# Loads, scale steps, filler products and the written-out order at the start of a fused attention and MLP kernel

## The chip, the core and the metric

The kernel runs on one core of a Trainium2 chip. The metric is the device time in microseconds of one execution. The notes use the profile's short names: PE is the matrix engine, DVE the vector engine, ACT the scalar engine, POOL the general-purpose engine, SP the queue that issues most DMAs.

## The reference

One input `x` (2048 tokens of 512 numbers) goes through a layer norm and then through two branches whose results are added to `x`. Branch A is attention with 32 heads of 16, in 4 segments of 512 tokens, with a memory carried from segment to segment. Branch B is a second layer norm and an MLP with 1792 hidden numbers.

```python
for s in range(N):
    qs, ks, vs = q[:, :, s], k[:, :, s], v[:, :, s]
    p = _softmax(qs @ ks^T * scale + mask)           # causal, inside the segment
    a_dot = p @ vs
    num, den = phi(qs) @ M, phi(qs) @ z + 1e-6       # memory of the segments before
    outs.append(g * num / den + (1.0 - g) * a_dot)
    M, z = M + phi(ks)^T @ vs, z + sum(phi(ks))
A = concat(outs) @ wo
B = gelu(layernorm(xn) @ w1 + b1) @ w2 + b2          # 512 -> 1792 -> 512
return x + A + B
```

## The kernel before, in words

Matrix work is done in pairs of 16-bit numbers: a value is split in a high and a low part, and a product is three matmuls (high by high, high by low, low by high; `split3`, L583). Before a weight can be split it is scaled by a power of two that follows from its sum of squares. The sum comes from ACT squares (`w_square`, L351) or from the trace of a product on PE (`w_trace`, L380 on PE, L382 on DVE); `qk_scale` and `w_scale` add it up over the partitions with a product by ones (L394, L412), take the exponent bits on DVE (`exponents`, L386) and form the factors from them (`power`, L390); `w_split` makes the high part on ACT (L445) and the low part on DVE (L446), or spreads the piece over POOL, ACT and POOL (L448, L450, L452). Raw weights lie in the same buffer as the split ones, two pieces further on.

The work is cut in steps with short names, and a step's instructions are issued when its key comes up. The tokens are handled in halves of 256 rows, `X` (load, statistics, root on POOL, normalization; L472, L483, L532, L534) and `Xt` (transposition, L561 on PE, L564 on ACT, L565 on DVE). A unit `i` is one segment and one group of 8 heads, 16 units in all. `Tp` is the product of q or k of unit 0 with the first 256 rows, `T` the product with the rest or with all 512; `V` is the product for v of 128 rows (12 matmuls of 512 columns). `M` (L741 on PE, L748 on DVE) finds the row maxima of unit `i`'s logits in 10 jobs, `R` turns them (L754 on PE), and they go through DRAM into the operand of `S` (L783, exponentials on ACT, L790). `pv` (L817) multiplies by v, `D` and `e` (L583 with w1, and L926) are the MLP's two layers, `out` (L944, added on DVE in L947) the last product, and `st` the store. `W` are products of the identity with itself that nobody reads (L501). `C` and `Cb` form the rows that undo the first layer norm's scale (L510, L524, L525).

The order is written out by hand in the string ORDER: each character names a stream of steps, and the next step of that stream is issued. So every engine runs its instructions in the order in which the string names their steps, and every DMA of SP likewise. The string BANKS gives each product its PSUM bank.

Of the kernel before, what the change touches and what calls it, by code (L numbers as in the profile page):

```python
# [19 lines left out]
P = 128  # L20
D = 512
# [11 lines left out]
NW = 8  # L33
# [25 lines left out]
def streams():  # L59
# [15 lines left out]
    for m in PARTS:  # L75
        put("loads", *[("wl", m, k) for k in range(LOADS[m])])
        if m == "qk":
            put("loads", ("hold",))
        if m == "v":
            put("loads", ("par",))  # L80
# [57 lines left out]
    "oamakrkkhbckkkk0h0bihehceddhff220ff22qhjkk2n1h1662gkkrp6237s7lg3k783w8th88999!x9u#k!w7#9$4$vRRv9R$9!3#R!#%k4J5"  # L138
    "WxkR%&RRzzz%(S%%Lz&WTzXU%Vst)L(uzz3%Tk)U&LvVYY(zTvU)z)VTz&L)Y(UYi3-YzVY*YYYk*K+-,X4zzyz**J5Y+YYYz-,6AAY-*5RAAA"
    "aBRB-RzzCBC.K.+C*C/,*A.+kAzRRR,zAA:WkRzAWz/.sRt.uzSy:TjRBwUBxBR.C.CCVCvDAbATEBFGAURwAvVARBRHxJYz/zCBCCTUICKzXA"  # L140
    "zYYzA:/VcYTURAzzsXBAz:VtiAYBvBSYYRzTzCCUuCCdDYvYz;YeEYVJT;FUVRfyRYfRY;;aATAzYbRUAzGAVYTBRcYAHzzdUBVBYeIYRSzz<z"
    "YYCCCKCz=AzYYYff>TUYYYAaAzjBsAAVtz<bYROBR<wTuyCNBCxCCA=AvDUY>RBREJPsVTYYFUGVTAuAvAHYtiwYzBzCxCBCICAzYNYRUAzAVB"
    "RYAzAvRzzzcvBCOSCBTUCCzzRYYLRDVYYEzFYzz<GzyYLYLHezATUIAMZAAAVQLBzBBWzCTCXKCCUzVAzdMJAzzsAAAMRBzMByBtCCuTCKCADA"
    "EPOwBFxAAvAvRNYZfYZfYBGUQRJBRYWCiVHKCICCzAYYzAAYBRAAzBSOYPXYYBzzzTsYzUztCuCaCCzzVYTwjxRUVTDRYYvbRzERUvVJFTURcY"
    "yWdYORYRYYSYNzeAAVYRiYTYBXYAzzYYRZUYAzAGYVRBTzzCKHBCIUCCAABVTzRWRAAXzRAUzzffRYBjVYYYTSzUQYysPBaVCCCtCADAEYBYwu"
    "AFTAGAYYxNYYBYBYQYCHCvObCICAAARvPJURABzBABszzzCCtCCLVuLTzcUVDvzzwxETdLeFzzzLGfRYYzfRHNUyVRTUVYRAAAYBRvYAAzIYMY"
    "ZBzzCBCCSKiCRAWzzaMYTYUAVzARJYbzcABABMQBYzzTUzZCCVCCTUKXsuMzYJRtDRPEyWwFxYAAAYYVGHTRQYUAABOvNIVYBRPBCCKXvCCAZA"
    "zYBYYzAAYBRAzzSjBesTzzzCCtduCUVCTDYURYYREwYzzvzxVYRTFGYJYUVYfYzRNZTyUVYYvRHRYYAAABYRYOfzAWzYSYYTYRUzAzBYYRQzzC"
    "IBCCCVzzAszAtTzURRYVAATAROWPvBUzRwRNBYyVYSXROBYCCTUXCVxCDTjAAYYYEYAFAABYGRYRYBRBHKvCIUCCCAzVATYzYYizzAsBzUzAVR"
    "QzARRTzBzBzCtCSCCPUDwLYExFYVvzGLyTYLNvLHIAAAMYzUAVzTYUYMzBzAYVMZQzZzzBCTCUOBCCAAstzzzYYYPwBWYzYAAABYVxYZNyvYBM"  # L150
    "CTCUCCvAABAYRRRDAEAzVBRFBGHRRQPWRCTCCICAjzAYUYsztAAWYXYVYzzAwvxzzBSzBXCBCTCUCDYVYTUYVYTvURYEzzVRTRYYNRRZzRRYYS"
    "FOYzUVzyATYYRUzAAGBVYYYYTHABXAzRBYUzzCCIVCCzzTAYRYUWVzAARYAzTARYBUVzBRRCSCBTUCCQDEXyVYYAAYTYFYGABPYABAYYBYHYCC"
    "UICCYAVAABYATYYBYAQUYYBCVCTUCCDEVYFYYGHYYIYYYYYYMMMZMZZZ"
# [4 lines left out]
    "01234567012345614526371052671034261705342617035426107356420735264071526540715402675430125673012657320614527036"  # L158
    "41752036475126347512034715623471625437164325741362534612054612704631720476231547361204367120436712430624751062"
    "41705241705617205436172436017236017620347620341576203145762031457632145176320475163204751632407513624057136240"  # L160
    "57162401572431507243107624531762541736257431602576403157640315640371564072561473265104765104736510427651024702"
    "63517305264137052641702614702351470623154706234710536427153642751036427513642735167340516735401564730215643725"
    "61437516437054317605431760543761054361205437205413725024513740256137425061742506314506310473152047361052170365"
    "27052431670524315627053614270361423761024671025671032567120536127410253645130243510624351067243167524316754236"
    "17542356417023564127035641270356120356142705164270514521670421657210465201476537206143720614206173540267302547"
    "03251403142650314261540356410235641027536142753641275036127503461250"
# [17 lines left out]
def infini_mixer_kernel(ctx: ExitStack, tc: tile.TileContext, x, wq, wk, wv, wo, beta, w1, b1, w2, b2, out):  # L184
# [71 lines left out]
    def col(j):  # L256
        return sc[:, j:j + 1]
# [25 lines left out]
    def w_load(m, k):  # L283
# [27 lines left out]
        elif m[0] == "1":  # L311
            f0, n = (0, FH) if m == "1a" else (FH, FH - 2)
            d = flat("1")[:, 1024 + 512 * f0:1024 + 512 * (f0 + n)].rearrange("p (f k c) -> p f k c", f=n, k=KT)
            for r in (2 * k, 2 * k + 1):
                Q.dma_start(d[:, :, r, :], w[P * r:P * r + P, P * f0:P * (f0 + n)].rearrange("p (f c) -> p f c", f=n))
        else:
            f0, n = {"v": (0, 2), "o": (0, 2), "2a": ((0, 4), (4, 3))[k % 2], "2b": (FH, FH - 2)}[m]
            Q.dma_start(flat(m[0])[:, 1024 + 512 * f0:1024 + 512 * (f0 + n)].rearrange("p (k c) -> p k c", k=n),
                        w[P * f0:P * (f0 + n), :].rearrange("(k p) c -> p k c", p=P))
# [5 lines left out]
    def w_square(m, k):  # L325
# [5 lines left out]
        else:  # L331
            to = am[:, AM[m] + k:AM[m] + k + 1]
            a = m[0]
            if m == "1a" and k == 2:
                r, to = b1t, am[:, 16:17]
            elif m[1:] == "a":
# [18 lines left out]
    def w_trace(m, k):  # L355
# [5 lines left out]
        else:  # L361
# [3 lines left out]
            else:  # L365
                r = flat(m[0])[:, 1024:1024 + 512 * FH].rearrange("p (b c) -> p b c", c=P)
                if m == "1a":
                    r = r.rearrange("p (f r) c -> p f r c", r=KT)[:, :, 2 * k:2 * k + 2]
                else:
                    r = r[:, (0, 16)[k]:(16, 28)[k]]  # L370
# [21 lines left out]
    def qk_scale(g0, n):  # L392
        p = dense()
        T.matmul(p[:, :2], ones, am[:, :2 * NG].rearrange("p (w g) -> p w g", w=2)[:, :, g0:g0 + 1], start=True, stop=True)  # L394
        h = sm.tile([P, 2], F32, name="fa")
# [10 lines left out]
    def w_scale(m):  # L406
# [8 lines left out]
        a = sm.tile([P, 2], F32, name="fa")  # L415
# [22 lines left out]
    def w_split(m, n, k):  # L438
# [4 lines left out]
        h, l = WT[w][:, c, 0, :], WT[w][:, c, 1, :]  # L443
# [32 lines left out]
    def norm_root(h):  # L476
# [5 lines left out]
        if h == 0:  # L482
            G.tensor_tensor(r[:, 0], a[:, 0], mhalf[:, :2], op=OP.pow)  # L483
        G.tensor_scalar(a[:, 1], ag[:, :, 1], 1.0 + EPS, EPS * EPS, op0=OP.mult, op1=OP.add)
        if h == 0:
            G.tensor_tensor(r[:, 3], a[:, 1], mhalf[:, :2], op=OP.pow)
            nws[h] = ag, a
            return
# [3 lines left out]
        nws[h] = ag, a  # L492
# [3 lines left out]
    def warm(n):  # L496
# [3 lines left out]
        for k in range(4):  # L500
            T.matmul(p[:, :256], b[:, :P], b, start=k == 0, stop=k == 3)  # L501
# [4 lines left out]
    def ratio(h):  # L506

        a = nws[h][1][:, 0]
        c = stats[:, h % 4, 2]
        G.tensor_tensor(c, a, stats[:, h % 4, 0], op=OP.mult)  # L510
# [18 lines left out]
    def norm_apply(h, j, t):  # L529
        r = stats[:, h % 4]  # L530
        if h == 0:
# [327 lines left out]

    def save(tok):  # L860
        Q.dma_start(out[P * tok:P * tok + P, :], acc[tok])
# [8 lines left out]
    def d_job(j, f):  # L870
# [5 lines left out]
        split3(p[:, 256 * (f % 2):256 * (f % 2) + 256], lambda k, a: WT["1"][:, fo, a, P * k:P * k + P],  # L876
# [58 lines left out]
    def out_jobs(s):  # L935
        def f(b):
            def go():
                tok = 4 * s + b
                p = dense()
                i = 0  # L940
                for g in range(NG):
                    o = oT[NG * s + g]
                    for u, v in ((0, 0), (0, 1), (1, 0)):
                        T.matmul(p, o[:, u, P * b:P * b + P], wos[:, g, v, :], start=i == 0, stop=i == 3 * NG - 1)  # L944
                        i += 1
                t = acc[tok]
                V.scalar_tensor_tensor(t, p, col(CO), t, op0=OP.mult, op1=OP.add)  # L947
# [100 lines left out]
```

## Time and profile before

| | before |
|---|---|
| median of 3 runs | 692.51 us (691.97 to 692.7) |
| profiled execution | 692.55 us, of which the span from first to last instruction is 690.8 us |
| PE busy | 680.1 us, 98% of the span |
| DVE busy | 504.6 us, 73% |
| ACT busy | 472.2 us, 68% |
| POOL busy | 353.1 us, 51% |
| mean granted PE clock | 0.994 |

Busy times are unions of the engine's instructions as the profiler recorded them; ends of matmuls are modelled. A row of the timeline gives the start, the busy time of a merged group, the engine, line and operation, and in brackets the idle time before it with what ended it.

### The profile page before, as it was taken

Reading aid. Unit: us, or ns where it says so; the run is one execution under the profiler, and the core shown is the slowest. Engines: PE = TensorE matmul, PEld = TensorE weight load, DVE = VectorE, ACT = ScalarE, POOL = GpSimd, SP = SyncE. Lnnn points to the kernel's source line nnn. Section 1 sums busy time; section 2 is a strip of 40 time slices with the busy share of each in tenths; the row PEclk is TensorE's granted clock in tenths of the full one; section 3 lists DMA queues with packets and bytes.
Section 4 is the critical chain, followed back from the end, with each engine's and each line's share of the span. In section 5 each row is a group of like instructions: output and inputs, shape, how many; then the busy total and the mean of one; then the engine's idle time right before and its main releaser. Section 6 shows DMA issues by size and latency. Waiting matters only on the chain.

```text
span 690.8 us, 15856 instructions
## 1 busy us (share of the span) xinstructions
PE 680.1 (98%) x5855; PEld 393.0 (57%) x5855; DVE 504.6 (73%) x1612; ACT 472.2 (68%) x877; POOL 353.1 (51%) x577
## 2 busy tenths in 40 slices
PE   6999999999999999999999999999999999999997
PEld 5854655657654566755546555565555447465543
DVE  5899978897787669867696786968577475688622
ACT  3688897987766577668836738667865555767970
POOL 7488649575535343564554345434462405438562
PEclk8999999999999999999999999999999999999999
DMA  9888233302321142322221224221402113420101
GB/s 269 264 207 205 97 94 58 99 30 76 76 47 40 34 116 58 107 48 79 69 70 26 77 57 101 70 64 44 105 18 56 55 48 94 102 77 17 18 2 61
DMA packets 52745, 55.84 MB, mean 81 GB/s; under 512 B 4974, under 2 KB 41596, under 8 KB 52668
## 3 DMA queue, kind: packets, MB, share of 16 engines
q1 hardware_dynamic: 50364, 50.64, 26.4%
q0 software_dynamic: 2304, 4.20, 3.8%
q8 instruction: 46, 0.75, 0.5%
q14 instruction: 31, 0.25, 0.1%
HBM read 37.77 MB, written 17.05 MB: 79 GB/s over the span
## 4 chain that ended last, share of the span: by engine, by line
PE 96%; POOL 1%; DVE 1%; issue 0%; POOLq 0%
PE dense L583 40%; PE dense L926 21%; PE dense L817 11%; PE dense L944 6%; PE dense L783 6%; PE dense L741 6%; PE dense L681 2%; PE dense L561 1%; PE dense L380 1%; PE dense L697 1%; PE dense L648 1%; DVE dense L748 1%; PE dense L718 1%; DVE w1s L446 0%; PE dense L754 0%; POOL kst L237 0%
## 5 line engine op out<-in xcount | busy, mean ns | idle before, releaser
L748 DVE CUSTOM_DVE_ANT_0 dense<-dense,mask 128x384 f32<-128x384 f32 (+3 forms) x512 | 233.8, 526 | 39.0 <-PE dense L741 34.4
L790 ACT ACTIVATE pt<-dense,qkcs 128x512 f32<-128x512 f32 (+1 forms) x384 | 204.0, 632 | 35.0 <-PE dense L783 35.0
L926 PE MATMUL dense<-w2s,hT 128*128 128x512 f16 x672 | 166.0, 380 | 0.0
L583 PE MATMUL dense<-xnT,w1s 128*128 128x256 f16 x1344 | 161.2, 273 | 0.0
L804 POOL TENSOR_SCALAR_AFFINE_SELECT pt<-pt 128x256 f32<-128x256 f32 x256 | 102.3, 436 | 108.8 <-ACT pt L790 108.3
L583 PEld LDWEIGHTS <-w1s 128*128 128x128 f16 x1344 | 129.5, 98 | 29.2 <-issue 5.4
L900 POOL TENSOR_TENSOR hT<-hh,hT 128x512 f16<-128x512 f32 x64 | 68.3, 1067 | 95.8 <-ACT hT L898 89.2
L926 PEld LDWEIGHTS <-hT 128*128 128x128 f16 x672 | 61.0, 98 | 67.3 <-issue 13.4
L817 PE MATMUL dense<-pt,vt 128*32 128x512 f32 (+3 forms) x1024 | 77.6, 436 | 0.0
L748 DVE DVE_READ_ACCUMULATOR2_ANT mc<- 128x1 f32 x512 | 72.6, 142 | 0.0
L880 DVE SCALAR_TENSOR_TENSOR hT<-dense,sc,cb 128x512 f32<-128x512 f32 x64 | 43.6, 681 | 34.2 <-PE dense L583 27.7
L898 ACT ACTIVATE hT<-hh 128x512 f16<-128x512 f32 x64 | 37.4, 584 | 27.1 <-POOL hh L896 27.1
L817 PEld LDWEIGHTS dense<-pt,vt 128*32 128x32 f32 x1024 | 30.7, 109 | 41.7 <-issue 31.8
L783 PE MATMUL dense<-qst,kst 50*128 50x384 f16 (+3 forms) x512 | 52.1, 298 | 1.1 <-DVE mc L748 1.1
L896 POOL TENSOR_SCALAR hh<-hT,sc 128x512 f32<-128x512 f32 x64 | 42.1, 658 | 21.2 <-ACT hT L886 17.9
L741 PE MATMUL dense<-kst,qst 48*128 48x384 f16 (+3 forms) x512 | 51.5, 298 | 0.0
L886 ACT ACTIVATE hT<-hT,b1t 128x256 f32<-128x256 f32 x112 | 46.4, 495 | 0.2
L848 POOL TENSOR_TENSOR nN<-nN,oT 128x512 f32<-128x512 f32 x16 | 21.0, 1312 | 49.5 <-DVE oT L660 49.5
L583 PE MATMUL dense<-xnT,wks 128*128 128x512 f16 (+1 forms) x252 | 44.5, 329 | 0.0
L583 PE MATMUL dense<-xnT,wqs 128*128 128x512 f16 (+1 forms) x252 | 44.4, 329 | 0.0
L944 PE MATMUL dense<-wos,oT 128*128 128x512 f16 x192 | 43.8, 379 | 0.0
L583 PE MATMUL dense<-wvs,xnT 128*128 128x512 f16 x192 | 43.8, 379 | 0.0
(230 smaller groups left out, 838.1 us busy)
## 6 DMA issues: line engine op xcount, KB each, us to landing
kst<-kd SPq DMA_DIRECT2D x32, 192.0 KB
qst<-qd SPq DMA_DIRECT2D x32, 192.0 KB
qd<-hl SPq DMA_DIRECT2D x36, 128.0 KB
kd<-hl SPq DMA_DIRECT2D x33, 128.0 KB
acc<-in_A_x_dram SPq DMA_DIRECT2D x16, 256.0 KB
acc<-in_B_b_dram POOLq DMA_DIRECT2D x16, 256.0 KB, 4.2
out_dram<-acc SPq DMA_DIRECT2D x16, 256.0 KB
xt<-in_A_x_dram SPq DMA_DIRECT2D x14, 256.0 KB
```

The lines of the kernel that those rows point to most:

```text
L583: T.matmul(p, ws(k, a), xs(k, b), start=i == 0, stop=i == 3 * KT - 1)
L741: T.matmul(p[:, o:o + n], stk[i, 0][r, t, P * qb:P * qb + P], stk[i, 1][r, t, :n], start=True, stop=True)
L748: V.tensor_tensor_reduce(p[:, o:o + n], p[:, o:o + n], mask[:, 512 - n:], 1.0, -3e38, OP.add, OP.max, mc[i][:, 4 * b + t, qb:qb + 1])
L783: T.matmul(p[:, o:o + n], stk[i, 1][r, t, P * kb:P * kb + P], stk[i, 0][r, t, P * kb:], start=True, stop=True)
L790: A.activation(pt[i, 4 * b + t][:, OFF[kb]:OFF[kb] + n], p[:, c:c + n], AF.Exp, scale=qkcs[:, 1, i % NG:i % NG + 1])
L804: G.affine_select(v, v, pattern=[[0, 2], [1, P]], compare_op=OP.is_ge, fill=0.0, base=0, channel_multiplier=-1)
L817: T.matmul(p[32 * c:32 * c + 32, P * kb:], vt[s, kb][:, 4 * g + c, 16 * odd:16 * odd + 32], pt[i, 2 * c + odd][:, OFF[kb]:OFF[kb] + LEN[kb ...
L880: V.scalar_tensor_tensor(hzs[fh][:, f0:f + 1, :], p[:, :256 * n].rearrange("p (f c) -> p f c", f=n), col(CG + fh), cbt[hf].unsqueeze(1).to ...
L886: A.activation(hzs[j % 2][:, f, :], hzs[j % 2][:, f, :], AF.Gelu_apprx_tanh, bias=b1t[:, fo:fo + 1])
L900: G.tensor_tensor(hT[:, z, 1, :], hht[j, c], hT[:, z, 0, :], op=OP.subtract)
L926: T.matmul(p, t[:, u, P * a:P * a + P], w2s[:, fo, v, :], start=fi == 0 and n == 0, stop=fi == FH - 1 and n == 2)
L944: T.matmul(p, o[:, u, P * b:P * b + P], wos[:, g, v, :], start=i == 0, stop=i == 3 * NG - 1)
```

## The change: what it does

The first loads are put in another order: one half of v's weights comes before the first pieces of q and k, the other half right behind them, and the second 256 rows of x come after all of q and k. With that the second half's normalization moves from POOL to DVE (`norm_apply`, `h < 2`), without the steps that only POOL needed. The loads of each weight are streams of their own, so ORDER can place them apart.

The exponent bits of a scale are written to PSUM (`p[:, 4:6]`, `p[:, 6:8]`) and not to a small tile in SBUF, and the factors are formed from there. A step `W` has 2 products and not 4, and there are 24 steps and not 8. Weight w1 is kept in rows of k (`krow`, `w1piece`): a row of its load is one piece of 896 or 640 numbers and not 7 or 5 pieces of 128. The last 128 rows are finished in two halves of 256 columns (`halves`): product, addition and store. ORDER and BANKS are new up to unit 3; the last 1189 steps stand in the order of before.

```diff
-NW = 8
+NW = 24
...
-        put("loads", *[("wl", m, k) for k in range(LOADS[m])])
+        put("load" + m.lower(), *[("wl", m, k) for k in range(LOADS[m])])
...
-    "oamakrkkhbckkkk0h0bihehceddhff220ff22qhjkk2n1h1662gkkrp6237s7lg3k783w8th88999!x9u#k!w7#9$4$vRRv9R$9!3#R!#%k4J5"
+    "ahhhhlkhx6lkukhbhchhdkh$hhkhlehh6f6hhafhh$hih7jhsm8$7%%8gm8g8%%8x8bRrtcde89Rff9wn&&9&vny&(z()(C+(!D!*oB()ACB*2"
...
+    def krow(o, n, k, f0, nf):
+        return flat("1").rearrange("p (k x) -> p k x", k=KT)[:, k:k + n, o + P * f0:o + P * (f0 + nf)]
+    def w1piece(f, a, k=None):
+        t = WT["1"].rearrange("p n a c -> p (n a c)").rearrange("p (k f a c) -> p k f a c", k=KT, f=FT, a=2)
+        return t[:, :, f, a] if k is None else t[:, k, f, a]
...
-            d = flat("1")[:, 1024 + 512 * f0:1024 + 512 * (f0 + n)].rearrange("p (f k c) -> p f k c", f=n, k=KT)
             for r in (2 * k, 2 * k + 1):
-                Q.dma_start(d[:, :, r, :], w[P * r:P * r + P, P * f0:P * (f0 + n)].rearrange("p (f c) -> p f c", f=n))
+                Q.dma_start(krow(256, 1, r, f0, n)[:, 0], w[P * r:P * r + P, P * f0:P * (f0 + n)])
...
-        h = sm.tile([P, 2], F32, name="fa")
+        h = p[:, 4:6]
         exponents(h, p[:, :2])
...
-        a = sm.tile([P, 2], F32, name="fa")
+        a = p[:, 6:8]
...
-        h, l = WT[w][:, c, 0, :], WT[w][:, c, 1, :]
+        h, l = (w1piece(c, 0), w1piece(c, 1)) if w == "1" else (WT[w][:, c, 0, :], WT[w][:, c, 1, :])
...
-        if h == 0:
+        if h < 2:
             G.tensor_tensor(r[:, 0], a[:, 0], mhalf[:, :2], op=OP.pow)
+            return
...
-        for k in range(4):
-            T.matmul(p[:, :256], b[:, :P], b, start=k == 0, stop=k == 3)
+        for k in range(2):
+            T.matmul(p[:, :256], b[:, :P], b, start=k == 0, stop=k == 1)
...
-        if h == 0:
+        if h < 2:
             V.tensor_scalar(t, t, nws[h][0][:, j, 0:1], r[:, 0, j:j + 1], op0=OP.subtract, op1=OP.mult)
         else:
             G.tensor_scalar(t, t, r[:, 0, j:j + 1], r[:, 1, j:j + 1], op0=OP.mult, op1=OP.add)
...
+    def halves(tok):
+        return (slice(0, 256), slice(256, 512)) if tok == 4 * NSEG - 1 else (slice(0, 512),)
     def save(tok):
-        Q.dma_start(out[P * tok:P * tok + P, :], acc[tok])
+        for c in halves(tok):
+            Q.dma_start(out[P * tok:P * tok + P, c], acc[tok][:, c])
...
-                V.scalar_tensor_tensor(t, p, col(CO), t, op0=OP.mult, op1=OP.add)
+                for c in halves(tok):
...
+                            T.matmul(p[:, c], o[:, u, P * b:P * b + P], wos[:, g, v, c], start=i == 0, stop=i == 3 * NG - 1)
...
+                    V.scalar_tensor_tensor(t[:, c], p[:, c], col(CO), t[:, c], op0=OP.mult, op1=OP.add)
```

The first DMAs on SP before. The tiles `xt`, `nN` and `nD` are rows of x, `wks`, `wqs`, `wvs`, `w1s` weights in place, and `pt` holds raw weights of q, k and v.

```order
L546 DMA xt<-in_A_x_dram 128x512 x2
L546 DMA nN<-in_A_x_dram 128x512
L546 DMA nD<-in_A_x_dram 128x512
L290 DMA wks<-in_A_wk_dram 128x4x128
L290 DMA wqs<-in_A_wq_dram 128x4x128
L290 DMA wks<-in_A_wk_dram 128x4x128
L290 DMA wqs<-in_A_wq_dram 128x4x128
```

The first DMAs on SP now.

```order
L563 DMA xt<-in_A_x_dram 128x512 x2
L328 DMA wvs<-in_A_wv_dram 128x2x512
L301 DMA wks<-in_A_wk_dram 128x4x128
L301 DMA wqs<-in_A_wq_dram 128x4x128
L321 DMA pt<-in_A_wv_dram 128x512 x2
L301 DMA wks<-in_A_wk_dram 128x4x128
L301 DMA wqs<-in_A_wq_dram 128x4x128
```

In both, 1 MB stands ahead of the first k piece. The rows `nN` and `nD` now come seven DMAs further on, behind the rest of q and k and two small loads.

On DVE before, from the first normalization to the first two low parts of k and q (`xnT` is x transposed and split, `fa` the exponent bits, `qksc` the factors of q and k):

```order
L532 TENSOR_SCALAR xt<-xt,ag,stats 128x512 x2
L565 SCALAR_TENSOR_TENSOR xnT<-dense_224,xnT 128x4x128
L565 SCALAR_TENSOR_TENSOR xnT<-dense_231,xnT 128x4x128
L386 TENSOR_SCALAR fa<-dense_248 128x2
L390 TENSOR_SCALAR qksc<-fa 128x2 x4
L403 TENSOR_TENSOR qkcs<-qksc 128x1
L404 SCALAR_TENSOR_TENSOR qkcs<-qksc 128x1
L565 SCALAR_TENSOR_TENSOR xnT<-dense_258,xnT 128x4x128
L565 SCALAR_TENSOR_TENSOR xnT<-dense_265,xnT 128x4x128
L382 SCALAR_TENSOR_TENSOR dense_238,am<-dense_238,ident 128x128
```

On DVE now, from the same place, up to k's low part:

```order
L549 TENSOR_SCALAR xt<-xt,ag,stats 128x512 x2
L582 SCALAR_TENSOR_TENSOR xnT<-dense_230,xnT 128x4x128
L402 TENSOR_SCALAR dense_237<-dense_237 128x2
L406 TENSOR_SCALAR qksc<-dense_237 128x2 x4
L419 TENSOR_TENSOR qkcs<-qksc 128x1
L420 SCALAR_TENSOR_TENSOR qkcs<-qksc 128x1
L582 SCALAR_TENSOR_TENSOR xnT<-dense_256,xnT 128x4x128
L398 SCALAR_TENSOR_TENSOR dense_198,am<-dense_198,ident 128x128
L462 SCALAR_TENSOR_TENSOR wks<-wks,qksc 128x512
```

The transposed second half (the last two `xnT` rows of before) no longer stands ahead of k's low part, and the factors stand between the two transposed tiles of the first half.

On ACT before, from the first transposed tile:

```order
L564 ACTIVATE xnT<-dense_224 128x4x128
L564 ACTIVATE xnT<-dense_231 128x4x128
L564 ACTIVATE xnT<-dense_258 128x4x128
L564 ACTIVATE xnT<-dense_265 128x4x128
L525 ACTIVATE cb<-dense_290 128x256
L445 ACTIVATE wks<-wks,qksc 128x512
L445 ACTIVATE wqs<-wqs,qksc 128x512
```

On ACT now, from the same place (`vt` is v in place for the later products):

```order
L581 ACTIVATE xnT<-dense_230 128x4x128
L581 ACTIVATE xnT<-dense_256 128x4x128
L461 ACTIVATE wks<-wks,qksc 128x512
L542 ACTIVATE cb<-dense_291 128x256
L461 ACTIVATE wqs<-wqs,qksc 128x512
L461 ACTIVATE wvs<-wvs,sc 128x512 x2
L461 ACTIVATE wvs<-pt,sc 128x512 x2
L725 ACTIVATE vt_85<-dense_384 128x16x2x16
L725 ACTIVATE vt_86<-dense_420 128x16x2x16
```

The first high part of k stands ahead of `cb`, the four pieces of v follow at once, and two of the four `V` products come here; before, the first `vt` stood behind the first gelu.

More of the change, by code (lines that the diff above doesn't have):

```diff
@@ L143 @@
[L143 to L152, printed above, removed]
```

84 lines of the change are left out of this document (51 added, 33 removed).

## The prediction

> **What bounds the kernel now.** I read the page first, then the busy time by stretches, then the timeline of the start, of the first row maxima and of the end. The page's first lines:
>
> ```profile
> span 690.8 us, 15856 instructions
> PE 680.1 (98%) x5855; PEld 393.0 (57%) x5855; DVE 504.6 (73%) x1612; ACT 472.2 (68%) x877; POOL 353.1 (51%) x577
> PE 96%; POOL 1%; DVE 1%; issue 0%; POOLq 0%
> ```
>
> The last row is the chain that ended last: 96% of it is PE. So the time is PE's work plus what PE idles, and the 10.7 us that it idles are few. The stretches tell where. I cut them at the first projection (18.3), at the first row maximum of unit 0 on DVE (41.45), at the last of unit 1 (89.1), and where the old and the new order become the same (168).
>
> ```profile
> 0.00:18.30 18.30, 12.85 (x88) 10.40 (x89) 10.54 (x30) 6.61 (x12) 13.12 (x35) 0.81 0.98 270
> 18.30:41.45 23.15, 23.13 (x231) 19.32 (x228) 19.86 (x60) 15.83 (x28) 14.05 (x14) 1.00 0.95 261
> 41.45:89.10 47.65, 46.59 (x401) 24.63 (x396) 45.46 (x170) 41.44 (x82) 32.96 (x42) 1.00 0.55 147
> 89.10:168.00 78.90, 78.90 (x745) 47.55 (x743) 62.77 (x199) 66.23 (x126) 51.11 (x88) 1.00 0.28 71
> 168.00:684.00 516.00, 515.96 (x4396) 290.08 (x4393) 364.43 (x1156) 342.12 (x633) 241.84 (x400) 1.00 0.24 61
> ```
>
> The columns are the length, then the busy time of PE, PE's weight loads, DVE, ACT and POOL, the granted clock, the DMA share and GB/s. Two things stand here. From 18.3 us on PE is full to the end. And from 41.45 to 89.1 DVE is full as well, 45.46 of 47.65 us: two engines with no room at once. What ends PE's poor start is therefore worth what DVE lets through, and after 168 us nothing moves but the last 128 rows.
>
> **The first projection.** These rows are the chain to it.
>
> ```profile
> 3.65 0.69 DVE L472 BATCH_NORM_STATS2 st<-xt 128x6 f32<-128x512 f32 x1 [2.72 <-DMA xt<-in_A_x_dram]
> 7.60 0.97 DVE L532 TENSOR_SCALAR xt<-xt,ag,stats 128x512 f32<-128x512 f32 x2
> 8.45 0.63 ACT L351 ACTIVATE wqs<-wqs 128x512 bf16<-128x512 f32 x1 [0.15 <-DMA wqs<-in_A_wq_dram]
> 8.98 0.19 ACT L351 ACTIVATION_READ_ACCUMULATOR wqs<-wqs 128x1 f32 x1
> 9.32 1.08 ACT L564 ACTIVATE xnT<-dense 128x512 f16<-128x512 f32 x2 [0.15 <-PE dense L561]
> 10.68 0.53 PE L394 MATMUL dense<-am,ones 128*128 128x2 f32 x2
> 11.44 1.70 DVE L390 TENSOR_SCALAR qksc<-fa 128x2 int32<-128x2 int32 x4
> 12.02 1.07 POOL L227 MEMSET vt<- 128x256 f32 x4
> 14.77 0.69 DVE L565 SCALAR_TENSOR_TENSOR xnT<-dense,xnT 128x512 f16<-128x512 f32 x1 [0.16 <-ACT xnT L564]
> 16.28 0.39 ACT L525 ACTIVATE cb<-dense 128x256 f32<-128x256 f32 x1 [1.53 <-PE dense L524]
> 16.56 0.71 ACT L445 ACTIVATE wks<-wks,qksc 128x512 f16<-128x512 f32 x1
> 17.52 0.75 DVE L446 SCALAR_TENSOR_TENSOR wks<-wks,qksc 128x512 f16<-128x512 f32 x1
> 18.34 1.47 PE L583 MATMUL dense<-xnT,wks 128*128 128x256 f16 x12
> 20.55 0.39 DVE L390 TENSOR_SCALAR qksc<-fa 128x6 int32<-128x6 int32 x4
> ```
>
> The factors of q and k are ready at 13.1 us, yet k's high part starts at 16.56: ACT runs in order and waits for `cb`, whose operand comes late from PE, and before that it copies the second half of x. The new order takes both out of the way. Its chain: 1 MB lies ahead of k's first piece as before, so q's lands by 8.45 and ACT's square with its read ends at 9.2. The sum over partitions is 0.53, to 9.8. DVE splits the first transposed tile in 0.69, from 9.95 to 10.65, then takes the exponent and four factors. Those four cost 1.70 us at 11.44, while POOL cleared `vt`, and 0.39 at 20.55, while it stood still; from PSUM I take 0.39, the nearer row to a read that POOL isn't part of, with 1.70 as the other end. That is 11.2. ACT's copy of the second tile ends at about 11.3, k's high part 0.71 later at 12.0, and DVE, after 0.69 for the second tile and 0.44 for v's trace, does the low part from 12.5 to 13.3. **The first projection moves from 18.34 to 13.3 us**, 5.0 earlier.
>
> The Trainium skill, "SBUF — State Buffer" (SBUF: two separate sides), says that DVE and GpSimd share a port pair as an exclusive lock, and "VectorE: DVE Perf Modes" (Why PSUM operands drop a tier) that a PSUM operand rules out the mode that takes both ports. The two rows above agree, 1.70 beside a memset and 0.39 without; by the rule 0.39 holds whatever POOL does, and the sum stays. The same rule speaks against the second half's normalization on DVE, SBUF to SBUF; that is part of the slower rival below.
>
> **From there to the row maxima.** What PE does ahead of unit 0's first job grows.
>
> ```profile
> 8.63 1.09 PE L561 MATMUL dense<-ident,xt 128*128 128x128 f32 x8 [2.76 <-DVE xt L532]
> 16.03 0.64 PE L380 MATMUL dense<-pt 128*128 128x128 bf16 x4
> 40.94 0.82 PE L741 MATMUL dense<-kst,qst 48*128 48x512 f16 x8
> 41.45 0.69 DVE L748 CUSTOM_DVE_ANT_0 dense<-dense,mask 128x512 f32<-128x512 f32 x1
> 41.70 2.76 PE L583 MATMUL dense<-wvs,xnT 128*128 128x512 f16 x12
> 47.53 2.75 PE L583 MATMUL dense<-wvs,xnT 128*128 128x512 f16 x12
> ```
>
> Before, 22.6 us of PE work lay between 18.34 and 40.94. Added to it are the first two v products, which stood at 41.70 and 47.53 (each 2.76 with its last end, 2.6 in a full stream), the transposes of the second half (0.9, from the 1.09 of eight), and 16 of the trace products of q and k that stood ahead of the first projection (16 at 0.06, 1.0); taken out are one group of unread products and a sum, 0.7. That is 29.0 us, so PE comes to unit 0's maxima at 13.3 + 29.0 = 42.3, not 40.94: the 5.0 us are spent on work that is done sooner, and the maxima start 1.4 us later.
>
> DVE is the other bound of that start. It was busy 10.54 + 19.86 = 30.4 of 41.45 us. It gains the two normalizations (0.97) and one low part of w2 that the order now puts ahead (0.75), and loses 1.3 on the factors: 30.8. Its waits were 11 us. The one for x, 3.6 with the idle start, stays; at most 1.5 of the others go. So DVE is there at 40.5 to 41.9, ahead of PE, and 42.3 holds. With PE's first job taking 0.5 to the first reduction as before, DVE starts at 42.8.
>
> From 41.45 to 89.1 DVE's work was 45.46. One low part (0.75) has gone ahead, and its waits there were 2.2, mostly for PE:
>
> ```profile
> DVE hT L880 <- PE dense L583: 0.8, 1, 0.8
> DVE mst L721 <- PE dense L718: 0.3, 1, 0.3
> DVE dense L748 <- PE dense L741: 0.2, 1, 0.2
> 88.77 1.47 PE L583 MATMUL dense<-xnT,w1s 128*128 128x256 f16 x12
> 90.08 0.27 PE L754 MATMUL dense<-ident,mc 128*32 128x128 f32 x1
> ```
>
> PE has less to do in this stretch now (both v products and what else went ahead, about 5.5 us), so it is mostly ahead and DVE waits less: I keep 0.6 of the 2.2. DVE ends unit 1's maxima at 42.8 + 44.7 + 0.6 = 88.1. The turn of these maxima stood at 90.08 because PE had a job of the MLP until then (88.77, 12 products), about 1 us after DVE was done. PE will now wait for DVE and go at 88.3. That is **1.8 us earlier**, and 3.2 of the 5.0 have turned into waits of PE for DVE. Behind the turn PE was full for 77.9 us to the common order, and the same work is left there; the 16.1 us that DVE idles there (62.77 busy of 78.90) leave it room. So 1.8 arrives at 168 and at the end.
>
> **The other parts.** The w1 load in long rows: SP spent
>
> ```profile
> 12.12 6.74 SPq L315 DMA_DIRECT2D w1s<-in_B_w_dram x4
> 18.90 2.30 SPq L318 DMA_DIRECT2D w2s<-in_B_w_dram x2
> 17.87 0.46 PEld L380 LDWEIGHTS <-pt 128*128 128x128 bf16 x8 [0.19 <-DMA pt<-in_A_wv_dram]
> ```
>
> 6.74 us on four loads of 448 KB in 512-byte pieces, and 2.30 on two of w2 (1.75 MB in 2 KB pieces). Both feed steps that PE reaches after 23 us in the new order, so I count nothing for them; were w1 as slow as before, its last piece would be about 1.7 us later and still come before its traces. The split pieces with 4 runs of 128 numbers are priced like the tiles of `xnT`, which are written that way in the same 0.69: nothing. The added unread products lie in PE's idle start, but for two steps (4 products, 0.4) that I have in PE's slack before the turn.
>
> The end:
>
> ```profile
> 675.89 10.74 PE L944 MATMUL dense<-wos,oT 128*128 128x512 f16 x48
> 686.67 0.75 DVE L947 SCALAR_TENSOR_TENSOR acc<-dense,sc,acc 128x512 f32<-128x512 f32 x1 [1.84 <-PE dense L944]
> 679.67 8.10 SPq L861 DMA_DIRECT2D out_dram<-acc x4
> ```
>
> The last addition ends at 687.42, and the span at 690.8: 3.4 us for the last store. The product in halves costs PE 24 matmuls of 256 columns for 12 of 512, the same columns. The last addition is half as wide, 0.75 to about 0.45, and its store half as long; the first half's addition and store go beside the second half's product. I take 0.3 + 0.3 = **0.6 us**, between 0.3 (a store whose time is all latency) and 1.0.
>
> The sum: 692.55 - 1.8 - 0.6 = 690.15 for the profiled execution, which stands within 0.05 of the median 692.51. Forecast 690.1.
>
> **The rivals.** *PE's whole lead arrives.* From the first projection to the turn PE took 71.7 us, full (18.34 to 90.08). The products that the new order puts there, each at its spacing in this trace, come to 0.6 less: the transposes and traces that came in are outweighed by steps of the MLP and projections that went behind the turn. If nothing waits, the turn is at 13.3 + 71.1 = 84.4 and, 5.6 earlier, the end at 692.55 - 5.6 - 0.6 = 686.4. For it: DVE was just not the bound before (the turn came 1 us after its last reduction). Against it: DVE would need unit 1's maxima done at 84.3, with 30.8 + 44.7 us of work and 3.6 us that it must wait for x, so about 5 us of other waits in all; before it had 9.6 (11 + 2.2 - 3.6).
>
> *Only the end arrives.* The clock: in this stretch it was halved while PE worked.
>
> ```profile
> 10.00:17.00 7.00, 5.79 (x36) 5.32 (x37) 5.01 (x14) 2.33 (x5) 4.78 (x10) 0.52 1.15 321
> ```
>
> PE had stood still for 2.8 us before (the bracket at 8.63). If the finer products don't keep the clock up, the two first projections and the traces run at half rate until about 16.6, which puts PE 1.5 to 2 us later at unit 0's maxima, and everything behind: 690.1 + 1.8 = 691.9. The Trainium skill, "TensorE: Matmul & The Clock Gate" (Part 1), says that about 3.4 us without activity halves the clock and as long a busy window restores it. The row agrees, and by that rule the new products, never 3 us apart, keep the full rate: the forecast.
>
> *Slower: the second half of x comes too late.* It is now loaded behind all of q, k and v, next to w1's 1.75 MB. Its chain after landing is the statistics (1.7), POOL's root (1.0), normalization on DVE (1.0) and transposition, and in the forecast, with landing at 16.9 (4 MB end with it, 14.8 us at the first stretch's 270 GB/s, counted from 2 us, between the first issue and the first landing), it is done 1.5 us before PE ends the two v products. v's last piece was awaited until 17.87 in the old order with 0.5 MB less ahead. If the tiles share the queues with w1 they land at 20 to 23 us. Each us beyond 18.4 delays unit 0's second projection, its row maxima and DVE's full stretch by one; from 20.8 on the kernel is slower than before, and at 23 it takes 690.1 + 4.6 = 694.7.
>
> **How the numbers follow.** A measurement of this kernel tells 0.2% (1.4 us) from no change. Chances: forecast 0.47 (its own range 688.6 to 691.0), whole lead 0.19, only the end 0.20, slower 0.14. So faster 0.66, same 0.20, slower 0.14. The range goes from 686.8, which leaves out half of the second case, to 693.4, which leaves out the larger part of the last.
>
> **What the profile would show.** Right: the first projection at 13 to 14 us, unit 0's first row maximum on DVE at 42 to 43.5, DVE busy over 95% from there to the end of unit 1's, PE idle by 2 to 4 us in that stretch with DVE's `mc` as the releaser, the turn at 87.5 to 89.5, and from there to 168 us of before the same distances. Wrong: the turn near 84.5 with no PE waits (DVE had more room than I counted), a granted clock of 0.5 past 14 us, a DVE wait for `nN` that ends after 19 us, or a last store as long as before.

## The result, and the profile after

| kernel | us, median | runs | range |
|---|---|---|---|
| before | 692.57 | 4 | 691.97 to 692.70 |
| after | 714.93 | 4 | 712.48 to 716.02 |

The ratio is 1.032 (95% interval 1.0289 to 1.035): slower by 22 us, where 2.4 us less was forecast. The profiled execution took 715.93 us. The first lines of its page and its chain of waits:

```profile
span 714.2 us, 15911 instructions
PE 687.7 (96%) x5883; PEld 397.3 (56%) x5883; DVE 500.7 (70%) x1615; ACT 473.7 (66%) x877; POOL 349.0 (49%) x574
PE 86%; DVE 6%; DMA 3%; POOL 2%; issue 1%; ACT 1%; SPq 0%; POOLq 0%; DVEq 0%; ACTq 0%
```

PE's share of the chain fell from 96% to 86%: other engines and a DMA are on it now. The busy time by stretches (columns as in the prediction) says where, cut at 18.3 and 41.45 as before and at unit 0's first row maximum (60.49) and the turn of unit 1's (112.28):

```profile
0.00:18.30 18.30, 15.62 (x125) 12.59 (x126) 9.34 (x28) 8.36 (x14) 8.65 (x24) 1.00 0.92 279
18.30:41.45 23.15, 16.94 (x144) 11.61 (x142) 13.23 (x49) 8.16 (x16) 6.60 (x12) 0.99 0.68 213
60.49:112.28 51.79, 47.64 (x360) 25.43 (x360) 44.27 (x170) 39.35 (x76) 32.03 (x45) 0.93 0.42 111
40.00:50.00 10.00, 0.00 (x0) 0.00 (x0) 1.02 (x3) 2.47 (x4) 2.88 (x3) 0.54 0.67 159
50.00:60.00 10.00, 9.82 (x72) 8.15 (x73) 6.05 (x11) 6.45 (x11) 5.31 (x7) 0.77 0.08 18
```

Up to 18.3 us the forecast holds: PE is busy for 15.62 us, 12.85 before. Then PE does nothing at all from 40 to 50 us, and works at a granted clock of 0.77 in the ten after. The timeline at the start, and at the row maxima and the turn:

```profile
12.20 0.36 DVE L406 TENSOR_SCALAR qksc<-dense 128x2 int32<-128x2 int32 x4
14.15 1.47 PE L600 MATMUL dense<-xnT,wks 128*128 128x256 f16 x12
60.49 0.82 PE L758 MATMUL dense<-kst,qst 48*128 48x512 f16 x8
112.28 0.27 PE L771 MATMUL dense<-ident,mc 128*32 128x128 f32 x1
```

The first projection came at 14.15 (18.34 before), but the row maxima at 60.49 and not 40.94, the turn at 112.28 and not 90.08. The timeline between shows what PE waits for, in brackets:

```profile
34.88 0.88 SPq L325 DMA_DIRECT2D w1s<-in_B_w_dram  x2
34.93 0.74 POOL L464 TENSOR_SCALAR w1s<-w1s,sc 128x512 f32<-128x512 f32 x1
41.04 0.63 ACT L466 ACTIVATE w1s<-w1s 128x512 f16<-128x512 f32 x1 [7.20 <-DMA w1s<-in_B_w_dram]
41.75 1.15 POOL L468 TENSOR_TENSOR w1s<-w1s 128x512 f16<-128x512 f32 x1 [6.08 <-ACT w1s L466]
42.93 0.83 SPq L325 DMA_DIRECT2D w1s<-in_B_w_dram  x2
45.93 0.72 ACT L461 ACTIVATE w1s<-w1s,sc 128x512 f16<-128x512 f32 x1 [3.78 <-DMA w1s<-in_B_w_dram]
46.69 0.75 DVE L462 SCALAR_TENSOR_TENSOR w1s<-w1s,sc 128x512 f16<-128x512 f32 x1 [10.85 <-ACT w1s L461]
47.47 0.63 ACT L466 ACTIVATE w1s<-w1s 128x512 f16<-128x512 f32 x1 [0.82 <-DVE w1s L462]
48.18 1.15 POOL L468 TENSOR_TENSOR w1s<-w1s 128x512 f16<-128x512 f32 x1 [5.28 <-ACT w1s L466]
49.43 0.69 POOL L464 TENSOR_SCALAR w1s<-w1s,sc 128x512 f32<-128x512 f32 x1
50.18 2.10 PE L600 MATMUL dense<-xnT,w1s 128*128 128x256 f16 x9 [12.28 <-POOL w1s L464]
```

Read it from below. A product of the MLP waits 12.28 us for a step that scales a piece of w1 on POOL (49.43). Ahead of this stand four more steps on w1, from 45.93 to 48.18, and the first of them has waited 3.78 us for the load issued at 42.93. That load is issued 0.03 us after POOL's step at 41.75 ends, this step waits for ACT's at 41.04, and that one has waited 7.20 us for the load issued at 34.88. All these steps are splits of w1's first half (column blocks 0 to 6), but both loads bring its second half (blocks 7 to 11). So load and split wait for one another in turn, though they touch no number in common.

The layout explains how they can look alike. A partition's w1 buffer is now 4 rows of 1792 words, one for each k. Column block f lies at words 128f (result) and 256 + 128f (raw) of every row. A split of block f so reaches from row 0 to row 3, with four runs of 128 and gaps between. The second half's raw words are 1152 to 1791 of each row: in rows 0, 1 and 2 they lie in those gaps. Before, a block was one run of 512 words and the second half lay behind the first. The theory: **what waits for what is decided by the stretch from a step's first to its last word**, so in the new layout splits of different blocks, products that read them and loads of the other half all count as overlapping. The rivals: the new order alone put the splits and the MLP's first products too early; the strided steps or the traffic of the load are slow in themselves. POOL's step at 34.93 is taken up below.

### The profile page after: what moved, and what is told of

The parts are those of the page before. It is cut to its first block, busy times and chain, and to the rows that moved or that the text cites. A ratio compares the mean times of both kernels' runs of the same rounds, so it can differ in the third digit from the quotient of the medians.

```text
span 714.2 us, 15911 instructions
## 1 busy us (share of the span) xinstructions
PE 687.7 (96%) x5883; PEld 397.3 (56%) x5883; DVE 500.7 (70%) x1615; ACT 473.7 (66%) x877; POOL 349.0 (49%) x574
## 4 chain that ended last, share of the span: by engine, by line
PE 86%; DVE 6%; DMA 3%; POOL 2%; issue 1%; ACT 1%; SPq 0%; POOLq 0%; DVEq 0%; ACTq 0%
PE dense L600 36%; PE dense L947 18%; PE dense L834 10%; PE dense L800 6%; PE dense L967 6%; PE dense L758 5%; DVE dense L765 3%; PE dense L698 2%; DMA w1s<-in_B_w_dram 1%; PE dense L578 1%; POOL w1s L468 1%; PE dense L714 1%; DMA wvs<-in_A_wv_dram 1%; PE dense L396 1%; PE dense L665 1%
## 5 line engine op out<-in xcount | busy, mean ns | idle before, releaser
L600 PE MATMUL dense<-xnT,w1s 128*128 128x256 f16 x1344 | 166.5, 278 | 17.6 <-POOL w1s L464 13.2
L600 PEld LDWEIGHTS <-w1s 128*128 128x128 f16 x1344 | 131.1, 99 | 50.5 <-POOL w1s L464 13.9
L901 DVE SCALAR_TENSOR_TENSOR hT<-dense,sc,cb 128x512 f32<-128x512 f32 x64 | 43.5, 679 | 43.9 <-PE dense L600 43.8
L765 DVE DVE_READ_ACCUMULATOR2_ANT mc<- 128x1 f32 x512 | 71.7, 140 | 0.0
L919 ACT ACTIVATE hT<-hh 128x512 f16<-128x512 f32 x64 | 37.3, 583 | 23.9 <-POOL hh L917 23.9
L967 PE MATMUL dense<-wos,oT 128*128 128x512 f16 (+1 forms) x204 | 44.0, 367 | 0.6 <-DVE acc L969 0.6
```

Of the source, the lines that this page charges most:

```text
L600: T.matmul(p, ws(k, a), xs(k, b), start=i == 0, stop=i == 3 * KT - 1)
L765: V.tensor_tensor_reduce(p[:, o:o + n], p[:, o:o + n], mask[:, 512 - n:], 1.0, -3e38, OP.add, OP.max, mc[i][:, 4 * b + t, qb:qb + 1])
L901: V.scalar_tensor_tensor(hzs[fh][:, f0:f + 1, :], p[:, :256 * n].rearrange("p (f c) -> p f c", f=n), col(CG + fh), cbt[hf].unsqueeze(1).to ...
L967: T.matmul(p[:, c], o[:, u, P * b:P * b + P], wos[:, g, v, c], start=i == 0, stop=i == 3 * NG - 1)
```

## The experiments

Times of the start and the end in each profiled execution; the kernels are told below.

| kernel | first projection | first row maxima (PE) | turn of unit 1 | span | median, us | ratio to before (95%) |
|---|---|---|---|---|---|---|
| before | 18.34 | 40.94 | 90.08 | 690.8 | 692.57 | |
| after | 14.15 | 60.49 | 112.28 | 714.2 | 714.93 | 1.032 (1.0289 to 1.035) |
| old layout | 15.48 | 44.68 | 88.59 | 690.0 | 691.05 | 0.9976 (0.9967 to 0.9986) |
| new layout, late load | 13.90 | 52.39 | 102.38 | 704.2 | 705.42 | 1.0186 (1.0171 to 1.0201) |
| before with new layout | 18.01 | 54.73 | 105.61 | 707.0 | 708.41 | 1.0231 (1.0214 to 1.0248) |
| late load, row 3 early | 14.28 | 52.94 | 102.85 | 705.0 | 705.51 | 1.0191 (1.0174 to 1.0208) |
| late load, products in the waits | 14.59 | 50.54 | 100.48 | 701.9 | 703.10 | 1.0154 (1.0140 to 1.0167) |

**Layout or order.** First the changed kernel with w1's old layout, and the old kernel with the new one. The main lines of the first edit (squares, traces and products follow them, and the second edit is the reverse in the old kernel):

```diff
-                Q.dma_start(krow(256, 1, r, f0, n)[:, 0], w[P * r:P * r + P, P * f0:P * (f0 + n)])
+                Q.dma_start(d[:, :, r, :], w[P * r:P * r + P, P * f0:P * (f0 + n)].rearrange("p (f c) -> p f c", f=n))
...
-        h, l = (w1piece(c, 0), w1piece(c, 1)) if w == "1" else (WT[w][:, c, 0, :], WT[w][:, c, 1, :])
+        h, l = WT[w][:, c, 0, :], WT[w][:, c, 1, :]
```

> The changed kernel with w1 kept in its old layout (512-byte pieces, one block of 512 numbers per column block); order, unread products, PSUM scale steps and halves stay. Theory, the layout (steps on the first half of w1 and the loads of its second half span the same stretch of SBUF with their four runs, and wait for each other): the PE waits for w1s between 30 and 60 us go, 691 us (688.5 to 694). Rival, the order (the first half's splits and the MLP's first products stand too early for any layout): the waits stay, 708 to 716. Rival, both: 697 to 706.

> The old kernel with only w1's layout changed to rows of k (load, squares, traces, splits, products). Theory, the layout: its second half's loads stand between the splits of column blocks 2 and 3 of the first half here too, so splits wait for them: slower, 700 us (696 to 708). Rival, the order: no loss without it, 691.5 to 693.

Measured: 691.05 us for the new order with the old layout, slightly faster than before; 708.41 for the old order with the new layout, just above the 696 to 708 expected. So the layout costs 15.7 us in the old order (against 692.72 for the kernel before beside it) and 23.9 in the new one, and the order by itself costs nothing. With the old layout the windows of the new order show PE full again:

```profile
18.30:41.45 23.15, 22.99 (x207) 17.29 (x206) 19.70 (x62) 13.36 (x26) 12.40 (x18) 1.00 0.81 226
41.45:89.10 47.65, 47.11 (x393) 27.13 (x391) 46.21 (x173) 42.99 (x83) 36.01 (x48) 1.00 0.64 161
```

**Which waits.** In the next kernel the two early loads of the second half stand behind the last split of the first:

```diff
-... ("ws","1a",0,2) ("wl","1b",0) ("Tr",0,1) ... ("A",0,0) ("wl","1b",1) ("ws","1a",5,0) ... ("ws","1a",6,2) ("D",0,3) ...
+... ("ws","1a",0,2) ("Tr",0,1) ... ("A",0,0) ("ws","1a",5,0) ... ("ws","1a",6,2) ("wl","1b",0) ("wl","1b",1) ("D",0,3) ...
```

> The changed kernel, new layout, with the two loads of the second half of w1 that fall between the splits of the first half moved behind the last of these splits. Theory, the layout, loads: no engine waits for a w1 load between 30 and 50 us, and most of the 24 us goes; the splits still wait for one another (POOL for ACT, ACT for POOL, DVE for ACT), which was 4 to 8 us of PE's waits: 698 us (692 to 703). Rival, the chain of splits alone carries the loss: 708 to 715. Rival, the loads alone: 690 to 692.

Measured: 705.42 us, 9.5 less than the changed kernel, and no engine waits for a load of w1 from 18 to 60 us. The other 14.4 us are still there; that is more than the 692 to 703 expected, so the splits' waits for one another had been priced too low. Its timeline from 28 us, the first steps on w1's first half and the product that waits longest:

```profile
28.02 0.69 POOL L464 TENSOR_SCALAR w1s<-w1s,sc 128x512 f32<-128x512 f32 x1 [2.96 <-PE dense L430]
28.75 0.72 ACT L461 ACTIVATE w1s<-w1s,sc 128x512 f16<-128x512 f32 x1 [0.41 <-POOL w1s L464]
29.61 0.74 DVE L462 SCALAR_TENSOR_TENSOR w1s<-w1s,sc 128x512 f16<-128x512 f32 x1
30.39 0.63 ACT L466 ACTIVATE w1s<-w1s 128x512 f16<-128x512 f32 x1 [0.92 <-DVE w1s L462]
31.11 0.69 POOL L464 TENSOR_SCALAR w1s<-w1s,sc 128x512 f32<-128x512 f32 x1 [2.40 <-ACT w1s L466]
31.84 0.72 ACT L461 ACTIVATE w1s<-w1s,sc 128x512 f16<-128x512 f32 x1 [0.33 <-POOL w1s L464]
41.60 2.10 PE L600 MATMUL dense<-xnT,w1s 128*128 128x256 f16 x9 [3.23 <-POOL w1s L464]
```

And the same steps with the old layout:

```profile
29.61 1.36 POOL L448 TENSOR_SCALAR w1s<-w1s,sc 128x512 f32<-128x512 f32 x2 [2.96 <-PE dense L414]
29.82 0.72 ACT L445 ACTIVATE w1s<-w1s,sc 128x512 f16<-128x512 f32 x1
30.43 0.63 ACT L450 ACTIVATE w1s<-w1s 128x512 f16<-128x512 f32 x1
31.14 1.16 POOL L452 TENSOR_TENSOR w1s<-w1s 128x512 f16<-128x512 f32 x1 [0.17 <-ACT w1s L450]
31.19 1.65 DVE L446 SCALAR_TENSOR_TENSOR w1s<-w1s,sc 128x512 f16<-128x512 f32 x1
```

In the first, one step begins only when the one ahead is done, on whatever engine: 28.02, 28.75, 29.61, 30.39, 31.11, 31.84. By the order of the steps these belong to column blocks 0, 1, 1, 0, 2 and 3. In the second, ACT starts 0.21 us after POOL, DVE and POOL run at once. The median durations of these steps are the same in both layouts (ACT 0.63 and 0.72 us, DVE 0.75, POOL 0.69 and 1.16), so the strided access itself costs these steps nothing; that rival is out.

**Stretch or traffic.** Row 3 of the second half starts at word 3 x 1792 + 1152, just behind the last word of block 6. It alone was put where the changed kernel loads rows 0 and 1, and the other three behind the last split:

```diff
-            for r in (2 * k, 2 * k + 1):
+            for r in (2 * k, 2 * k + 1) if m == "1a" else ((3,), (0, 1, 2))[k]:
```

> New layout; of the four row blocks of w1's second half only the last (k = 3) is loaded where the changed kernel loads k = 0 and 1, the other three behind the last split of the first half. Its words lie behind the last word that any column block of the first half touches, the others' between their runs. Theory, what waits is decided by the stretch from a step's first to its last word: no split waits for that load, 705.4 us as with all four late (704 to 707). Rival, any load into w1's buffer, or its traffic, delays the splits: 708 to 712.

Measured: 705.51 us, as with all four late.

```profile
34.97 0.45 SPq L325 DMA_DIRECT2D w1s<-in_B_w_dram  x1
```

No wait for this load stands among the waits of 18 to 60 us, and the step of ACT that came at 41.04 in the changed kernel comes at 35.84. It is one row in place of two, so half the traffic. A load of the same buffer at the same place is harmless when it lies behind the stretch. The kernels above show that the layout makes steps wait that share no number; that rows 0 to 2 are waited for because of the stretch, and not for some other trait of them, is shown only by this contrast.

And the stretch is not the whole rule. POOL's step at 34.93 in the changed kernel scales block 4 in place, comes behind the load of rows 0 and 1 in the order, and has these rows within its stretch. Yet it began 0.05 us after that load was issued, while the next step, ACT's, waited for the load until 41.04. POOL's step and the load both handle 32-bit words only. In every pair of the rows above that did wait, one of the two reads or writes the 16-bit results. Whether that is the missing condition no run tested.

**The clock.** In the kernel with the late load PE waits 8.1 us for steps on w1, and the loss is 14.4.

```profile
PE dense L600 <- POOL w1s L464: 4.1, 3, 3.2
PE dense L600 <- POOL w1s L468: 4.0, 2, 2.1
```

A part could be the clock, which is at 0.50 there from 37 to 46 us. So PE was given something to do in two of these waits:

```diff
         p = dp[0]
+        for k in range((16, 24)[f] if j == 0 and f < 2 else 0):
+            b = ident.bitcast(BF)
+            T.matmul(p[:, 256 * f:256 * f + 256], b[:, :P], b, start=k % 2 == 0, stop=k % 2 == 1)
```

> New layout, late load of the second half, and 16 and 24 unread matmuls of 256 columns ahead of the first two products of the MLP, where PE otherwise stands still for the splits (1.8 and 2.7 us of PE at full clock, inside waits of 2.1 and 3.2 us). Theory, a part of the loss is the clock, which falls to 0.5 from 37 to 46 us while PE waits and works: 702.7 us (701.5 to 703.7), 2.7 less than without. Rival, the loss is the waits alone: 705.4 to 707.

Measured: 703.10 us, 2.3 less (ratio 1.0154 against 1.0186, intervals apart). More work for PE, and less time. The stretch from 42 to 46 us, without the products and with them; ahead of the last two columns stands the clock:

```profile
42.00:44.00 2.00, 2.00 (x12) 1.56 (x11) 0.26 (x1) 0.00 (x0) 0.00 (x0) 0.50 0.00 0
44.00:46.00 2.00, 2.00 (x11) 1.44 (x10) 1.43 (x6) 1.22 (x3) 1.16 (x2) 0.50 0.00 0
```

```profile
42.00:44.00 2.00, 1.68 (x16) 1.53 (x17) 0.48 (x1) 0.00 (x0) 0.27 (x1) 1.00 0.00 0
44.00:46.00 2.00, 2.00 (x21) 1.78 (x19) 1.42 (x6) 1.43 (x3) 1.37 (x2) 1.00 0.03 8
```

In the last of these stretches 11 matmuls run in 2 us against 21. So 2.3 of the 14.4 us went when the clock stayed up. If that and the 8.1 us of waits add, 4.0 are left that no run places. By the trace, 7.7 us of the loss lie ahead of the first row maxima (52.39 against 44.68 with the old layout) and 6.1 between them and the turn (50.0 against 43.9). There PE still waits 2.2 us for steps on w1, 1.9 of them for a split of the second half. The late loads may have a part in the rest: SP issues them at 48.25, and the stores of `ame` behind them start at 50.08 (40.86 with the old layout).

**The small terms.** Four edits of the kernel with the old layout, and one of the old kernel.

```diff
-    return (slice(0, 256), slice(256, 512)) if tok == 4 * NSEG - 1 else (slice(0, 512),)
+    return (slice(0, 512),)
```

> The changed order with w1's old layout, and the last 128 rows again in one product, one addition, one store. Theory, the halves bring nothing (in the trace of the changed kernel with the old layout the second half's product waits 0.58 us for the first half's addition, and 3.4 us lie between the last addition and the end of the span, as before): 690.7 us, 0.3 less than with the halves (690.2 to 691.1). Rival, the prediction's term: 0.6 more, 691.65.

```diff
-                p = dense()
                 t = acc[tok]
                 for c in halves(tok):
+                    p = dense()
```

> The changed order with w1's old layout, and the two halves of the last 128 rows in two PSUM tiles in place of one. Theory, the wait of PE for DVE comes from the shared tile: 690.45 us, 0.6 less than with the one tile. Rival, the time behind the last product is the store's and starts no sooner: 691.05, no difference.

The second also needs one more bank in BANKS. Measured: 691.83 (0.9989, 0.9980 to 0.9997) with the last rows whole, 691.13 (0.9979, 0.9967 to 0.9991) with the halves in two tiles. Both medians lie nearer the rival than the theory, but the intervals overlap, with each other and with 0.9976; by totals the tail can't be told. The traces can, counted from the third addition to the end of the span: 6.72 us before (690.8 - 684.08), 7.16 whole in the new order (689.3 - 682.14), 7.23 in halves, 6.48 in halves with two tiles. The two other traces of the old order have 6.73 and 6.82, the six others of halves in one tile 7.21 to 7.26. The 7.16 stands apart: there the span ends 3.8 us after the last addition, in the eleven other traces 3.4 to 3.5. The rows of halves in one tile, then in two:

```profile
682.77 0.75 DVE L953 SCALAR_TENSOR_TENSOR acc<-dense,sc,acc 128x512 f32<-128x512 f32 x1 [1.84 <-PE dense L951]
684.61 1.47 PE L951 MATMUL dense<-wos,oT 128*128 128x256 f16 x12 [0.58 <-DVE acc L953]
686.12 0.48 DVE L953 SCALAR_TENSOR_TENSOR acc<-dense,sc,acc 128x256 f32<-128x256 f32 x1 [1.56 <-PE dense L951]
```

```profile
681.52 0.75 DVE L953 SCALAR_TENSOR_TENSOR acc<-dense,sc,acc 128x512 f32<-128x512 f32 x1 [1.84 <-PE dense L951]
684.14 0.48 DVE L953 SCALAR_TENSOR_TENSOR acc<-dense,sc,acc 128x256 f32<-128x256 f32 x1 [0.83 <-PE dense L951]
```

In one tile the second half's product waits 0.58 us until the first half's addition has read its own columns. In two tiles, in one trace, the wait is gone and 0.7 us with it. Columns 0 to 255 and 256 to 511 don't overlap even as stretches, so this is another kind of wait than that in w1's buffer; the runs show only that it comes with the shared tile.

```diff
-        h = p[:, 4:6]
+        h = sm.tile([P, 2], F32, name="fa")
...
-        a = p[:, 6:8]
+        a = sm.tile([P, 2], F32, name="fa")
```

> The changed order with w1's old layout, and the intermediate value of the scales in SBUF again, not in PSUM. Theory, four factors of q and k take 1.7 us beside POOL's clears, not 0.36, and all behind it comes 1.3 us later: 692.3 us (691.8 to 692.9). Rival, the other work of DVE and ACT hides it, or POOL's clears lie elsewhere in this order: 691.05 (690.8 to 691.4).

> The old kernel with only the intermediate value of q's and k's scales in PSUM. Theory, an operand in PSUM keeps DVE's four factors out of the wait beside POOL's work: they take 0.36 to 0.40 us at 11.4 us, where they took 1.70 beside POOL's normalization and clears; the time stays (the wait of ACT for cb is later): 692.5 us within 0.2%. Rival, the wait comes with POOL whatever the operand: 1.70 again.

The second is the line of `h` the other way round, in the old kernel. Measured: 691.57 (0.9994, 0.9984 to 1.0003), between the ranges of theory and rival, and 692.31 (1.0003, 0.9994 to 1.0012), as expected. First the four factors of the new order from SBUF, then the old kernel's from PSUM, with what POOL does beside them:

```profile
11.29 0.38 DVE L390 TENSOR_SCALAR qksc<-fa 128x2 int32<-128x2 int32 x4
```

```profile
11.64 0.76 POOL L534 TENSOR_SCALAR nN<-nN,stats 128x512 f32<-128x512 f32 x1
11.94 0.36 DVE L390 TENSOR_SCALAR qksc<-dense 128x2 int32<-128x2 int32 x4
```

Beside POOL's normalization the factors take 0.36 us from PSUM, where the prediction's row had 1.70 from SBUF (beside the normalization too, and then the clears). The Trainium skill, "VectorE: DVE Perf Modes" (Why PSUM operands drop a tier), says that a PSUM operand rules out the mode that takes both of DVE's read ports; the 0.36 agrees. But in the new order POOL stands still then (its last clear ends at 10.8), and 0.38 comes from SBUF too: the order had already taken away what the edit avoids. The theory held in the old kernel and failed in the new one.

```diff
-            T.matmul(p[:, :256], b[:, :P], b, start=k == 0, stop=k == 1)
+            T.matmul(p[:, :16], b[:, :P], b[:, :16], start=k == 0, stop=k == 1)
```

> The changed order with w1's old layout, and each unread matmul of the start cut from 256 columns to 16. Theory, the clock: without them PE counts as idle, the granted clock is 0.5 for most of 8 to 17 us, unit 0's row maxima and the end come 1.5 us later: 692.5 us (691.8 to 693.5). Rival, they only fill PE: clock as before, 691.05 or up to 0.5 less, since the first transposes queued behind them.

Measured: 691.61 us (0.9993, 0.9984 to 1.0001), first projection at 14.40, turn at 87.86, both between those of the other kernels in this layout. The time lies below the theory's range and above the rival's, and tells nothing more. First the stretches from the start (the clock stands ahead of the last two columns), then two rows of PE:

```profile
1.60:7.80 6.20, 0.53 (x20) 0.43 (x17) 2.64 (x6) 0.47 (x1) 4.89 (x11) 1.00 0.88 257
7.80:13.00 5.20, 4.87 (x49) 4.44 (x50) 1.68 (x9) 2.91 (x7) 2.84 (x5) 1.00 1.17 316
```

```profile
10.89 1.09 PE L562 MATMUL dense<-ident,xt 128*128 128x128 f32 x4
11.93 1.01 PE L380 MATMUL dense<-pt 128*128 128x128 bf16 x8
```

The profile says 1.00, but its first record of the clock stands only at 14.1 us here; ahead of it the profile counts full speed with no record. The durations tell more: these four transposes and eight trace products take 0.60 and 0.62 us in the changed kernel at 11.15 and 12.02, behind its own first record at 10.2. So PE did run at about half rate up to some 14 us, as the theory had it; that this costs 1.5 us at the end is what didn't show.

Of the kernels run, the one with the old layout and two tiles for the halves is the one to take: 691.13 us, faster than before by 0.1 to 0.3% and than the changed kernel by some 3%. Whether it beats the same kernel with one tile by its 0.7 us stays open in the totals.

## Why the prediction was wrong, step by step

The step that failed is the one on w1: "Both feed steps that PE reaches after 23 us in the new order, so I count nothing for them", and "The split pieces with 4 runs of 128 numbers are priced like the tiles of `xnT` ... nothing". The prices are right, load and splits take as long as assumed or less. What was missed is that a new layout also changes which steps wait for which. No rival had it, and the list of signs of failure did not either. Its size: 714.93 - 691.05 = 23.9 us; 9.5 of it went with the early loads of the second half, and 14.4 stayed, the chain of splits with the clock (2.3) and 4.0 that no run places.

With the layout taken out, the other terms can be judged on the old-layout kernel. Its profiled execution took 691.72 us; the sum had been 690.15.

- *First projection 13.3.* 14.15 in the changed kernel, 13.03 to 15.48 in those with the old layout; here 2.2 late. Of this, 1.7 is the landing of q's piece (its square began at 10.13, not 8.45). The same first loads came later in the new order: k's square began at 7.82 to 9.24 in its nine traces, at 7.26 to 7.88 in the three of the old order. The rest is the clock, see below.
- *29.0 us of PE work from there to the maxima.* 44.68 - 15.48 = 29.2; 29.7 with two tiles. Right.
- *46.0 us from the maxima to the turn, DVE the bound* (88.3 - 42.3). 88.59 - 44.68 = 43.9, mis-sized by 2.1 us, and by its mechanism: the waits of PE for DVE, into which 3.2 us of the lead were to turn, didn't come. PE was busy for 43.37 of the 43.91 us and waited for no `mc`; DVE was busy for 43.16, 1.5 less than counted:

```profile
44.68:88.59 43.91, 43.37 (x360) 24.05 (x360) 43.16 (x169) 39.26 (x77) 32.55 (x46) 1.00 0.61 160
```

- *Nothing moves behind the turn but the end.* From the turn to the third addition of the last group 594.0 us before (684.08 - 90.08), 594.2 after (682.77 - 88.59). Right.
- *Last 128 rows, 0.6 less.* 0.5 more by the trace (7.23 against 6.72), since product and addition shared a tile. Mis-sized by 1.1, and the store's half gave nothing that can be seen.

2.2 + 0.2 - 2.1 + 0.2 + 1.1 = 1.6, the distance from 690.15 to 691.72. So the turn at 88.3 against 88.59 is right in part by luck: a late start and waits that didn't come cancelled. In the trace with two tiles, where the first projection came at 13.03, the turn came at 86.80.

The rival in which PE's whole lead arrives had this right: PE hardly waited. But it put PE's time from the first projection to the turn at 71.1 us, and PE was busy for 72.4 to 72.8 in the five kernels with the old layout. (It also called PE full in the 71.7 us of before, where it was busy for 70.67.)

The clock's rival came in part, and the prediction's reading of it was wrong. It said that the row of before agrees with an idle time of 3.4 us, but that row's wait was 2.8, and that products never 3 us apart keep the full rate. In two of the kernels with the old layout a wait of 2.5 us for a load was followed by a clock of 0.50 from 9.3 to 12.7 and from 7.9 to 11.3. In four others of the new order, the changed kernel among them, the clock's first record stands at 10.1 to 14.1 us. In these six the first projection came 5.7 to 6.4 us behind the start of k's square, in the three others 5.2: about 1 us of the start.

The rival of the late second half of x did not come: DVE waited for no load of it. (Its 4 MB are 4.19 million bytes in the table's units, so 15.5 us and not 14.8; nothing hung on that.)

## What to carry to other kernels

A new layout is more than its durations: for each step list which stretch of the buffer it spans, and ask which other steps fall into that stretch, loads above all. Here that named the waits to look for, though one step in the stretch did not wait. Interleaved pieces of one tile that are filled, changed and read at different times can become one long chain, even where no element is shared; two halves of one PSUM tile can wait for one another too. When such a kernel stalls, follow the brackets back from the waiting engine until a releaser comes up that has no business there, and move or separate that one first.

## What was not expected of the hardware

- In the kernel with the late load the clock fell to 0.50 at 36.7 us, after waits of PE of 2.11 and 0.56, with 1.5 us of work in the 3.4 us before. It came back at 46.9, behind 3.4 us in which PE was busy throughout. A wait of 3.2 us lay in between. 40 unread matmuls in the waits kept it at 1.00 and made the kernel faster.
- In every trace here the stretches at 0.50 between two records of the clock last 3.41 us or a multiple (6.83, 10.24, 13.65). The Trainium skill, "TensorE: Matmul & The Clock Gate" (Part 1), speaks of a free-running window of about 3.4 us, and that length agrees. But it puts the fall behind an idle window, and here the 3.4 us ahead of the fall were not idle.
- At the start the profile's 1.00 is no measurement: its first record of the clock stands at 10.2 us in the changed kernel. Eight trace products took 1.03 us ahead of it, at 7.13, and eight later ones 0.62.
